# Unused matmuls ahead of the last block, and a kernel's last 64 columns in a bank of their own

## The chip, the cores and the metric

The kernel runs on one core of a Trainium2 chip. The metric is the device time of one execution in microseconds (us). Before the change the median of three runs is 773.96 us (773.9 to 774.07).

## The reference

One decode step of a parallel block: attention with cached keys and values, and a feed-forward net, both on the same normalised input, summed with the input. Two batch rows, model width 1024, 32 query heads on 4 key/value heads of width 128, 32768 cached positions, feed-forward width 3584, all in f32:

```python
xn = _layernorm(x)
q  = (xn @ wq)                              # 2 x 32 heads x 128
p  = softmax(q . k_cache * 128 ** -0.5)     # over 32768 positions, 8 heads share one k, v
a  = (p . v_cache) @ wo                     # 4096 -> 1024
h  = silu(xn @ w1)                          # 1024 -> 3584
return x + a + h @ w2                       # 3584 -> 1024
```

## The kernel before

Every weight and cache element is used for at most a few rows, so the program is a stream of 331 MB through three SBUF buffers (bufA, bufB, bufC, each 128 x 16384 f32), issued by SyncE (SP) in one fixed order, with TensorE following. First come wq and w1 (query and hidden activations), then eight turns of a TensorE loop (one for each pair of key/value head and batch row) over keys and values, and last wo and w2, which this change concerns.

In this last stage the reduction over 4096 + 3584 = 7680 inputs is cut into 60 tiles of 128 inputs, numbered t = 0 to 59: 32 of wo (weights oT from the attention), 28 of w2 (weights hT). Each tile has 128 x 1024 weights. Tiles 0 to 15 lie in bufA, 16 to 31 in bufC, 32 to 47 in bufB, and 48 to 59 in bufA again. The stationary operand is 32 columns wide (two batch rows, padded), so a matmul fills one group of 32 output partitions, and several matmuls with different groups are in the array together.

`tiles()` (from L351) goes through a block. Up to t = PAIRED - 1 a tile is *paired*: it is cut into two halves of 512 columns, even tiles go to groups 0 and 1, odd ones to groups 2 and 3 of the PSUM bank acc2 = ps[0]. After tile PAIRED - 1 VectorE adds these sums to the input x into ob (L363). From t = PAIRED on a tile is cut into four quarters of 256 columns (QW), one for each group of the bank acc. The sums in ob are folded into acc by four matmuls with a 0/1 matrix (fold), which wait for VectorE.

The last tile, t = 59, comes in four transfers of 128 KB, each with 64 columns of all four quarters; w2 is laid out on the host so that each is contiguous. TensorE waits for each. Then ScalarE copies acc (128 x 256) to SBUF (L388), issues the store of every sixteenth row (8 rows of 1 KB, L389), waits for it and clears the semaphores (L393).

The order of the work is that of the written program on each engine; engines wait for each other on semaphores (`pe.wait`, `act.wait`, `sp.wait_ge`). SP issues the last eight transfers into bufA once TensorE is through with bufA's wo block.

Of the kernel before, what the change touches and what calls it, by code (L numbers as in the profile page):

```python
# [3 lines left out]
F32 = mybir.dt.float32  # L4
# [4 lines left out]
B, HQ, HKV, SK, DH, D, F = 2, 32, 4, 32768, 128, 1024, 3584  # L9
P = 128  # L10
REP = HQ // HKV
W = 16384
# [4 lines left out]
FT = F // P  # L17
QW = D // 4
# [36 lines left out]
def gqa_plus_mlp_kernel(nc, x, kt, v, wq, wo, w1, w2, out):  # L55


    pe, dve, act, pool = (Stream(nc, e, n) for e, n in
                          ((nc.tensor, "pe"), (nc.vector, "dve"), (nc.scalar, "act"), (nc.gpsimd, "pool")))
    sp = nc.sync  # L60
    sems = [pe.sem, dve.sem, act.sem, pool.sem]

    def sem(name):
        sems.append(nc.alloc_semaphore(name))
        return sems[-1]

    def sb(name, *shape):
        return nc.alloc_sbuf_tensor(name, shape, F32).ap()

    def bank(name):  # L70
        return nc.alloc_psum_tensor(name, (P, 512), F32).ap()

    bufA, bufB, bufC = (sb(n, P, W) for n in ("bufA", "bufB", "bufC"))
    ldA, ldB, ldC, ldx, ldr, done = (sem(n) for n in ("ldA", "ldB", "ldC", "ldx", "ldr", "done"))
    tq, tps, trm, tgd, te, tls, tob = (sem(n) for n in ("tq", "tps", "trm", "tgd", "te", "tls", "tob"))
    ident, ones, sel, fold = sb("ident", P, P), sb("ones", P, P), sb("sel", P, 32), sb("fold", P, 64)
# [7 lines left out]
    oT, hT = sb("oT", P, HQ, 32), sb("hT", P, FT, 32)  # L84
    pre, sig, rsig = (sb(n, P, FT, B) for n in ("pre", "sig", "rsig"))
    pr = [sb(f"pr{i}", P, 512) for i in range(2)]
    ob, ot = sb("ob", P, 512), sb("ot", P, QW)
# [4 lines left out]
    pair = [nc.alloc_psum_tensor(f"ps{i}", (P, 1024), F32).ap() for i in range(NC)]  # L92
    ps = [pair[a // 2][:, a % 2 * 512:(a % 2 + 1) * 512] for a in range(2 * NC)]
    po, acc, smA, smB = (bank(n) for n in ("po", "acc", "smA", "smB"))
    acc = acc[:, :QW]

    def mm(o, lhsT, rhs, start=True, stop=True):
        return nc.tensor.matmul(o, lhsT, rhs, start=start, stop=stop)  # L98
# [26 lines left out]
    for i in range(2):  # L125
        t = dve.mark(V.bn_stats(stats[:, i, :], xt[:, i * 512:(i + 1) * 512]))
    dve.wait(t)
    t = dve.mark(V.bn_aggr(mv, stats))
    var, std, y0, t0, t1, rstd = (ln[:, i:i + 1] for i in range(6))
    dve.wait(t)  # L130
    t = dve.mark(V.tensor_scalar_add(var, mv[:, 1:2], EPS))
    act.wait(t)
    t = act.mark(nc.scalar.activation(std, var, AF.Sqrt))
    for f in (lambda: V.reciprocal(y0, std), lambda: V.tensor_mul(t0, y0, y0), lambda: V.tensor_mul(t1, t0, var),
# [4 lines left out]
        t = dve.mark(f())  # L139
    dve.wait(i_ident)  # L140
    i_sel = dve.mark(V.tensor_reduce(sel, ident.rearrange("p (g m) -> p m g", g=4), AX.X, ALU.add))
    i_fold = dve.mark(V.tensor_add(fold, ident[:, :64], ident[:, 64:]))
    pe.wait(t, i_ident)
    px = smA[:, :KT * B].rearrange("p (k b) -> p k b", b=B)
    for k in range(KT):
        m = mm(px[:, k, :], xn[:, k * P:(k + 1) * P], ident[:B, :B])
    t = pe.mark(m)
# [57 lines left out]
    def load(buf, src, s, *ticks):  # L205
        for of, n in ticks:
            sp.wait_ge(of.sem, n)
        sp.dma_start(buf, src).then_inc(s, 16)  # L208
# [5 lines left out]
    t = act.mark(nc.scalar.activation(sig, pre, AF.Exp, scale=-1.0))  # L214
    for f in (lambda: V.tensor_scalar_add(sig, sig, 1.0), lambda: V.reciprocal(rsig, sig),
              lambda: V.tensor_mul(hT[:, :, ::16], pre, rsig)):
        dve.wait(t, zs)
        t = dve.mark(f())
# [6 lines left out]
    start = pe.n  # L225
# [21 lines left out]
    for it in range(LOOPS):  # L247
        h, b = divmod(it, B)
        for c in range(NC):
            dve.wait(tick(it, c))  # L250
            t = dve.mark(V.transpose(st[:, 2 * c:2 * c + 2].rearrange("p a j m -> p (a j m)"), pair[c]))  # L251
            dve.wait(t)
            m = V.tensor_reduce(mx[:, c, :], st[:, 2 * c:2 * c + 2].rearrange("p a j (r m) -> p m (a j r)", r=4),  # L253
                                AX.X, ALU.max)
            if c == 0:
                m.then_inc(tps, 1)
        m = dve.mark(m)
# [5 lines left out]
        t = dve.mark(V.tensor_reduce(gm, smA[:REP, :P], AX.X, ALU.max))  # L263
# [3 lines left out]
        t = dve.mark(V.tensor_copy(gmax[:, 0, :], smB[:, :REP]))  # L267
# [6 lines left out]
        for c in range(NC):  # L274
            dve.wait(tick(it, 4 + c))
            m = V.tensor_reduce(ls[:, c, :], e8[c].rearrange("p n m -> p m n"), AX.X, ALU.add)  # L276
# [6 lines left out]
        t = dve.mark(V.reciprocal(rl, smA[:, :REP]))  # L283
# [8 lines left out]
    with nc.tensor.While(lambda: nc.tensor.snap(turn) < LOOPS):  # L292
        pe.take(tq)
        for a in range(4):
# [4 lines left out]
            for r in range(4):  # L299
                for q4 in range(4):  # L300
                    n = (4 * (a % 2) + q4) * 4 + r
                    m = mm(ps[a][32 * q4:32 * q4 + 32, :], qT[:, 32 * r:32 * r + 32], buf[:, n * 512:(n + 1) * 512],
                           r == 0, r == 3)
# [6 lines left out]
        for a in range(4):  # L310
# [4 lines left out]
            for j in range(16):  # L315
                q4, n = j % 4, 16 * (a % 2) + j
                m = mm(po[32 * q4:32 * q4 + 32, :], st[:, a, j, :], buf[:, n * 512:(n + 1) * 512],
                       a == 0 and j < 4, a == 3 and j >= 12)
# [5 lines left out]
        for r in range(4):  # L324
            m = mm(smB[:, :REP], ob[:, r * P:(r + 1) * P], sel[:, REP * r:REP * (r + 1)], r == 0, r == 3)
# [8 lines left out]
    def stream(buf, src, cuts, *ticks):  # L334

        for lo, hi in zip(cuts, cuts[1:]):
            s = sem(f"piece{len(pieces)}")
            load(buf[:, lo:hi], src[:, lo:hi], s, *ticks)
            pieces.append((hi, s))
            yield hi, s  # L340

    lo = 11 * D
# [3 lines left out]
        (bufB, [*stream(bufB, w2[:, :W], (0, 11 * D, W), tick(LOOPS - 1, 5))], 32),  # L346
    ]
    acc2 = ps[0]
    PAIRED = 56

    def tiles(buf, ends, at, n):  # L351
        for i in range(n):
            pe.wait((next(s for hi, s in ends if hi >= (i + 1) * D), 16))
            t = at + i
            lhsT, w = oT[:, t, :] if t < HQ else hT[:, t - HQ, :], buf[:, i * D:(i + 1) * D]
            if t < PAIRED:
                for half in range(2):
                    g = 2 * (t % 2) + half
                    m = mm(acc2[32 * g:32 * g + 32, :], lhsT, w[:, half * 512:(half + 1) * 512],
                           t < 2, t >= PAIRED - 2)  # L360
                if t == PAIRED - 1:
                    dve.wait(pe.mark(m), (ldr, 32))
                    i_sums = dve.mark(V.tensor_add(ob, acc2, xres))  # L363
            else:
                if t == PAIRED + 2:
                    pe.wait(i_fold, i_sums)
                    for j in range(4):
                        mm(acc[32 * j:32 * j + 32, :], fold[:, 32 * (j // 2):32 * (j // 2) + 32],
                           ob[:, (j % 2) * QW:(j % 2 + 1) * QW], False, False)
                for j in range(4):  # L370
                    m = mm(acc[32 * j:32 * j + 32, :], lhsT, w[:, j * QW:(j + 1) * QW], t == PAIRED, False)
        return m

    pe.wait(i_oT, i_hT)
    i_wo0 = pe.mark(tiles(*plan[0], 16))
    ends = [*stream(bufA, w2[:, W:], (0, 6 * D, 8 * D, 9 * D, 10 * D, lo, lo + QW, lo + 2 * QW, lo + 3 * QW,
                                      lo + D), i_wo0)]
    for buf, loaded, at in plan[1:]:
        tiles(buf, loaded, at, 16)
    tiles(bufA, ends, 48, 11)  # L380
    f = QW // 4
    for u in range(4):
        pe.wait((ends[5 + u][1], 16))
        for j in range(4):
            m = mm(acc[32 * j:32 * j + 32, u * f:(u + 1) * f], hT[:, FT - 1, :],
                   bufA[:, lo + (4 * u + j) * f:lo + (4 * u + j + 1) * f], False, u == 3)
    act.wait(pe.mark(m))
    act.wait(act.mark(nc.scalar.copy(ot, acc)))  # L388
    nc.scalar.dma_start(out, ot[::16, :]).then_inc(done, 16)  # L389
    act.wait((done, 16))  # L390
    first_sem = min(s.num for s in sems)
    assert sorted(s.num for s in sems) == list(range(first_sem, first_sem + len(sems)))
    nc.scalar.sem_clear(range(first_sem, first_sem + len(sems)))  # L393


# [27 lines left out]
```

## Time and profile before

| | us |
|---|---|
| median of 3 runs | 773.96 |
| the profiled execution | 773.65 |
| its span, first to last instruction | 772.2 |
| TensorE matmul busy | 386.6 (50%) |
| VectorE busy | 120.7 (16%) |
| ScalarE busy | 27.3 (4%) |
| data moved | 331.48 MB, mean 429 GB/s |

A row of a timeline reads: start, length, engine, line, operation, what it writes and reads, shape, number of records merged (x), and in brackets the idle time of the engine before it and what ended it. PE is TensorE's matmuls, PEld its weight loads, DVE VectorE, ACT ScalarE, a q behind a name the engine's sequencer. Line 98 is the helper that issues every matmul, so matmuls are told apart by the tiles that they write and read. The granted clock is the share of full speed at which TensorE runs.

### The profile page before, as it was taken

What the parts mean: (1) busy time and instruction counts of PE and PEld (TensorE: products, weight loads), DVE (VectorE), ACT (ScalarE), POOL (GpSimd) and SP (SyncE); (2) the same over time, 40 slices, a digit from 0 to 9 for tenths busy, and PEclk for the clock granted to TensorE, in tenths of its full rate; (3) what the DMA queues carried; (4) which work ended last, traced back from release to release, by engine and by line L of the source; (5) the groups of instructions that cost most, each with busy time, mean ns of one, the idle gap of its engine ahead of it and who ended that gap; (6) DMA issues with size and microseconds to landing.
All of it is one profiled execution on the core that took longest, in us unless ns stands there. A gap on an engine that the chain in (4) does not pass through costs nothing. (4 is left out here: it accounts for less than half of the span.)

```text
span 772.2 us, 5903 instructions
## 1 busy us (share of the span) xinstructions
PE 386.6 (50%) x2736; PEld 122.7 (16%) x2736; DVE 120.7 (16%) x153; ACT 27.3 (4%) x33; POOL 3.0 (0%) x10
## 2 busy tenths in 40 slices
PE   1545645554545444645454545444645454545466
PEld 1111211111111111211111111111211111111112
DVE  2000013111311131113111311131113111311000
ACT  0000101000100010001000000010001000000000
POOL 1000000000000000000000000000000000000000
PEclk9977677677677677677677677677677677677679
DMA  9999999999999999999999999999999999999997
GB/s 384 435 435 435 431 435 435 435 435 435 435 435 435 435 435 431 431 435 435 435 431 431 435 435 435 435 435 435 435 435 435 435 431 435 435 435 435 421 417 321
DMA packets 7091, 331.48 MB, mean 429 GB/s; under 512 B 798, under 2 KB 1318, under 8 KB 1708
## 3 DMA queue, kind: packets, MB, share of 16 engines
q1 hardware_dynamic: 7056, 331.35, 99.4%
q8 instruction: 6, 0.10, 0.0%
q10 hardware_dynamic: 28, 0.02, 0.0%
q14 instruction: 1, 0.01, 0.0%
HBM read 331.37 MB, written 0.01 MB: 429 GB/s over the span
## 5 line engine op out<-in xcount | busy, mean ns | idle before, releaser
L98 PE MATMUL ps<-bufB,qT 128*32 128x512 f32 x512 | 72.7, 731 | 83.2 <-PEq L52 83.2
L98 PE MATMUL po<-bufB,st 128*32 128x512 f32 x512 | 71.5, 721 | 82.7 <-PEq L52 82.7
L98 PE MATMUL ps<-bufA,qT 128*32 128x512 f32 x512 | 71.7, 723 | 53.1 <-PEq L52 53.1
L98 PE MATMUL po<-bufA,st 128*32 128x512 f32 x512 | 72.2, 727 | 39.3 <-PEq L52 39.3
L276 DVE TENSOR_REDUCE ls<-st 128x8 f32<-128x1024 f32 x16 | 31.8, 1984 | 229.6 <-PE po L98 229.6
L251 DVE STREAM_TRANSPOSE st<-ps 128x1024 f32<-128x1024 f32 x16 | 20.0, 1250 | 250.6 <-PE ps L98 250.6
L98 PEld LDWEIGHTS ps<-bufB,qT 128*32 128x32 f32 x512 | 20.0, 131 | 136.0 <-issue 136.0
L98 PEld LDWEIGHTS po<-bufB,st 128*32 128x32 f32 x512 | 19.7, 130 | 134.5 <-issue 134.5
L98 PEld LDWEIGHTS ps<-bufA,qT 128*32 128x32 f32 x512 | 19.8, 130 | 98.4 <-issue 98.4
L98 PEld LDWEIGHTS po<-bufA,st 128*32 128x32 f32 x512 | 19.9, 131 | 85.0 <-issue 85.0
L253 DVE TENSOR_REDUCE mx<-st 128x8 f32<-128x1024 f32 x16 | 31.7, 1981 | 0.6
L273 ACT ACTIVATE st<-st 128x1024 f32<-128x1024 f32 x16 | 16.9, 1056 | 358.7 <-DVE st L272 358.0
L98 PE MATMUL ps<-bufB,xnT 128*32 128x512 f32 x112 | 18.3, 730 | 14.8 <-PEq L52 14.8
L272 DVE TENSOR_TENSOR st<-st,gmax 128x1024 f32<-128x1024 f32 x16 | 18.9, 1222 | 0.3
L98 PE MATMUL smA<-ident,rm 128*8 128x128 f32 x16 | 3.7, 317 | 29.5 <-PEq L52 29.5
L98 PE MATMUL ps<-bufC,xnT 128*32 128x512 f32 x64 | 8.6, 698 | 10.8 <-DMA bufC<-in_w 10.8
L98 PE MATMUL ps<-bufC,oT 128*32 128x512 f32 x64 | 8.5, 692 | 9.7 <-DMA bufC<-in_wo 9.7
L281 ACT COPY ob<-po 128x512 f32<-128x512 f32 x8 | 4.7, 585 | 236.7 <-PE po L98 236.7
L98 PE MATMUL smA<-lsum,ones 128*128 128x8 f32 x16 | 3.3, 278 | 19.2 <-PEq L52 19.2
L98 PE MATMUL ps<-bufA,oT 128*32 128x512 f32 x64 | 9.6, 766 | 6.6 <-DMA bufA<-in_wo 6.6
L98 PE MATMUL ps<-bufA,xnT 128*32 128x512 f32 x64 | 9.7, 773 | 5.0 <-PEq L52 5.0
L98 PE MATMUL ps<-bufB,hT 128*32 128x512 f32 x64 | 8.9, 702 | 4.8 <-DMA bufB<-in_w 4.8
(65 smaller groups left out, 102.1 us busy)
## 6 DMA issues: line engine op xcount, KB each, us to landing
bufB<-in_w SPq DMA_DIRECT2D x1, 6144.0 KB, 26.2
bufB<-in_w SPq DMA_DIRECT2D x1, 5632.0 KB, 42.7
bufA<-in_w SPq DMA_DIRECT2D x1, 3072.0 KB, 36.3
bufB<-in_w SPq DMA_DIRECT2D x1, 2560.0 KB, 48.5
bufA<-in_w SPq DMA_DIRECT2D x3, 512.0 KB, 40.0
bufA<-in_w SPq DMA_DIRECT2D x1, 1024.0 KB, 38.4
bufA<-in_w SPq DMA_DIRECT2D x4, 128.0 KB, 38.0
bufA<-in_kt SPq DMA_DIRECT2D x8, 29.3
```

Of the source, the lines that this page charges most:

```text
L98: return nc.tensor.matmul(o, lhsT, rhs, start=start, stop=stop)
L251: t = dve.mark(V.transpose(st[:, 2 * c:2 * c + 2].rearrange("p a j m -> p (a j m)"), pair[c]))
L253: m = V.tensor_reduce(mx[:, c, :], st[:, 2 * c:2 * c + 2].rearrange("p a j (r m) -> p m (a j r)", r=4), AX.X, ALU.max)
L272: act.wait(dve.mark(V.tensor_sub(e8[c], e8[c], gmax.to_broadcast([P, 128, REP]))))
L273: nc.scalar.activation(e8[c], e8[c], AF.Exp, scale=SCALE).then_inc(te, 1)
L276: m = V.tensor_reduce(ls[:, c, :], e8[c].rearrange("p n m -> p m n"), AX.X, ALU.add)
L281: nc.scalar.copy(ob, po).then_inc(tob, 1)
```

## The change

Five edits, all in the last stage:

1. Between the block in bufB (tiles 32 to 47) and the last block in bufA, a TensorE loop of eight turns issues two matmuls a turn. Each multiplies 32 columns of the identity with pr[0] (128 x 512, f32) into partitions 0 to 31 of ps[2]. Nothing reads the result.
2. PAIRED is 57 in place of 56: tile 56 is paired as well. The fold matmuls stand ahead of tile 58, as before, but now ahead of that tile's wait for its transfer.
3. The 256 columns of a quarter are cut 192 + 64 (CUT = 192). Columns 0 to 191 go to acc, 192 to 255 to a second bank, smB (used by the attention before). Each quarter of tiles 57 and 58 and of the fold is thus two matmuls.
4. The last tile comes in two transfers, of 384 KB (the first 192 columns of each quarter) and 128 KB (the last 64). After the matmuls of each ScalarE copies that part.
5. SP issues the store, waits for it and clears the semaphores, in place of ScalarE. It stores every eighth row (16 rows), and the host takes every second of those.

```diff
-    PAIRED = 56
+    PAIRED, CUT = 57, 3 * QW // 4
+    banks = [(acc, 0, CUT), (smB, CUT, QW)]
+
+    def singly(j, lhsT, w, start=False):
+        for bank, a, e in banks:
+            mm(bank[32 * j:32 * j + 32, :e - a], lhsT, w[:, a:e], start, False)
 
     def tiles(buf, ends, at, n):
         for i in range(n):
+            t = at + i
+            if t == PAIRED + 1:
+                pe.wait(i_fold, i_sums)
+                for j in range(4):
+                    singly(j, fold[:, 32 * (j // 2):32 * (j // 2) + 32], ob[:, (j % 2) * QW:(j % 2 + 1) * QW])
             pe.wait((next(s for hi, s in ends if hi >= (i + 1) * D), 16))
...
             else:
-                if t == PAIRED + 2:
-                    pe.wait(i_fold, i_sums)
-                    for j in range(4):
-                        mm(acc[32 * j:32 * j + 32, :], fold[:, 32 * (j // 2):32 * (j // 2) + 32],
-                           ob[:, (j % 2) * QW:(j % 2 + 1) * QW], False, False)
                 for j in range(4):
-                    m = mm(acc[32 * j:32 * j + 32, :], lhsT, w[:, j * QW:(j + 1) * QW], t == PAIRED, False)
+                    singly(j, lhsT, w[:, j * QW:(j + 1) * QW], t == PAIRED)
...
-    ends = [*stream(bufA, w2[:, W:], (0, 6 * D, 8 * D, 9 * D, 10 * D, lo, lo + QW, lo + 2 * QW, lo + 3 * QW,
-                                      lo + D), i_wo0)]
+    ends = [*stream(bufA, w2[:, W:], (0, 6 * D, 8 * D, 9 * D, 10 * D, lo, lo + 4 * CUT, lo + D), i_wo0)]
     for buf, loaded, at in plan[1:]:
         tiles(buf, loaded, at, 16)
+
+
+    again = nc.tensor.alloc_register("again")
+    nc.tensor.reg_mov(again, 0)
+    with nc.tensor.While(lambda: nc.tensor.snap(again) < 8):
+        for i in range(2):
+            mm(ps[2][:32, :], ident[:, :32], pr[0])
+        nc.tensor.reg_add(again, again, 1)
     tiles(bufA, ends, 48, 11)
-    f = QW // 4
-    for u in range(4):
-        pe.wait((ends[5 + u][1], 16))
+    for (hi, landed), (bank, a, e) in zip(ends[5:], banks):
+        pe.wait((landed, 16))
         for j in range(4):
-            m = mm(acc[32 * j:32 * j + 32, u * f:(u + 1) * f], hT[:, FT - 1, :],
-                   bufA[:, lo + (4 * u + j) * f:lo + (4 * u + j + 1) * f], False, u == 3)
-    act.wait(pe.mark(m))
-    act.wait(act.mark(nc.scalar.copy(ot, acc)))
-    nc.scalar.dma_start(out, ot[::16, :]).then_inc(done, 16)
-    act.wait((done, 16))
+            at = lo + 4 * a + j * (e - a)
+            m = mm(bank[32 * j:32 * j + 32, :e - a], hT[:, FT - 1, :], bufA[:, at:at + e - a], False, True)
+        act.wait(pe.mark(m))
+        i_ot = act.mark(nc.scalar.copy(ot[:, a:e], bank[:, :e - a]))
+    sp.wait_ge(act.sem, i_ot[1])
+    sp.dma_start(out, ot[::8, :]).then_inc(done, 16)
+    sp.wait_ge(done, 16)
```

How the instructions stand on TensorE around the last block: first before, from the end of bufB's block (waits in brackets; pieceN is the semaphore of a transfer, dve is VectorE's).

```order
L98 MATMUL ps<-bufB,hT 32x512 x9
L98 MATMUL ps<-bufA,hT 32x512 [waits piece4]
L98 MATMUL ps<-bufA,hT 32x512 x11
L98 MATMUL ps<-bufA,hT 32x512 [waits piece5]
L98 MATMUL ps<-bufA,hT 32x512 x3
L98 MATMUL acc<-bufA,hT 32x256 [waits piece6]
```

The same place in the changed program:

```order
L97 MATMUL ps<-bufB,hT 32x512 x9
L386 UNCONDITIONAL_BRANCH
L386 COMPARE_AND_BRANCH
L97 MATMUL ps<-pr,ident 32x512 x2
L389 REGISTER_ALU
L386 UNCONDITIONAL_BRANCH
L97 MATMUL ps<-bufA,hT 32x512 [waits piece4]
L97 MATMUL ps<-bufA,hT 32x512 x11
L97 MATMUL ps<-bufA,hT 32x512 [waits piece5]
L97 MATMUL ps<-bufA,hT 32x512 x3
L97 MATMUL ps<-bufA,hT 32x512 [waits piece6]
L97 MATMUL ps<-bufA,hT 32x512
```

The loop (its body is run eight times) stands between bufB's last matmul and the wait for piece4, and tile 56 has become two paired matmuls behind piece6. At the end of ScalarE's program, before, there stood the copy, the store and the clearing of semaphores:

```order
L388 COPY ot<-acc 128x256
L389 DMA out_y<-ot 8x256
L393 ISA
```

Now ScalarE ends with two copies

```order
L397 COPY ot<-acc 128x192
L397 COPY ot<-smB 128x64
```

and SP's program ends with two transfers for the last tile in place of four, the store and the clearing:

```order
L207 DMA bufA<-in_w 128x768
L207 DMA bufA<-in_w 128x256
L399 DMA out_y<-ot 16x256
L403 ISA
```

More of the change, by code (lines that the diff above doesn't have):

```diff
@@ L94, in gqa_plus_mlp_kernel @@
     po, acc, smA, smB = (bank(n) for n in ("po", "acc", "smA", "smB"))
-    acc = acc[:, :QW]
     def mm(o, lhsT, rhs, start=True, stop=True):
@@ L348, in gqa_plus_mlp_kernel @@
     acc2 = ps[0]
-    PAIRED = 56
+    PAIRED, CUT = 57, 3 * QW // 4
[3 more added lines that the diff above has]
+            mm(bank[32 * j:32 * j + 32, :e - a], lhsT, w[:, a:e], start, False)
     def tiles(buf, ends, at, n):
         for i in range(n):
+            t = at + i
[3 more added lines that the diff above has]
+                    singly(j, fold[:, 32 * (j // 2):32 * (j // 2) + 32], ob[:, (j % 2) * QW:(j % 2 + 1) * QW])
             pe.wait((next(s for hi, s in ends if hi >= (i + 1) * D), 16))
-            t = at + i
             lhsT, w = oT[:, t, :] if t < HQ else hT[:, t - HQ, :], buf[:, i * D:(i + 1) * D]
@@ L375, in gqa_plus_mlp_kernel @@
     i_wo0 = pe.mark(tiles(*plan[0], 16))
-    ends = [*stream(bufA, w2[:, W:], (0, 6 * D, 8 * D, 9 * D, 10 * D, lo, lo + QW, lo + 2 * QW, lo + 3 * QW,
-                                      lo + D), i_wo0)]
+    ends = [*stream(bufA, w2[:, W:], (0, 6 * D, 8 * D, 9 * D, 10 * D, lo, lo + 4 * CUT, lo + D), i_wo0)]
     for buf, loaded, at in plan[1:]:
         tiles(buf, loaded, at, 16)
+    again = nc.tensor.alloc_register("again")
[4 more added lines that the diff above has]
+        nc.tensor.reg_add(again, again, 1)
     tiles(bufA, ends, 48, 11)
-    f = QW // 4
-    for u in range(4):
-        pe.wait((ends[5 + u][1], 16))
+    for (hi, landed), (bank, a, e) in zip(ends[5:], banks):
+        pe.wait((landed, 16))
         for j in range(4):
-            m = mm(acc[32 * j:32 * j + 32, u * f:(u + 1) * f], hT[:, FT - 1, :],
-                   bufA[:, lo + (4 * u + j) * f:lo + (4 * u + j + 1) * f], False, u == 3)
-    act.wait(pe.mark(m))
-    act.wait(act.mark(nc.scalar.copy(ot, acc)))
-    nc.scalar.dma_start(out, ot[::16, :]).then_inc(done, 16)
-    act.wait((done, 16))
+            at = lo + 4 * a + j * (e - a)
[5 more added lines that the diff above has]
+    sp.wait_ge(done, 16)
     first_sem = min(s.num for s in sems)
     assert sorted(s.num for s in sems) == list(range(first_sem, first_sem + len(sems)))
-    nc.scalar.sem_clear(range(first_sem, first_sem + len(sems)))
+    sp.sem_clear(range(first_sem, first_sem + len(sems)))
 def kernel(A_x, A_k_cache, A_v_cache, A_wq, A_wo, B_x, B_w1, B_w2):
@@ L413 @@
     last = arrays["w2"][:, -D:]
-    last[:] = lay(last, (P, 4, 4, QW // 4), (0, 2, 1, 3), (P, D))
+    groups, cut = last.reshape(P, 4, QW).copy(), 3 * QW // 4
+    last[:, :4 * cut], last[:, 4 * cut:] = groups[:, :, :cut].reshape(P, -1), groups[:, :, cut:].reshape(P, -1)
     nc = bacc.Bacc("TRN2", target_bir_lowering=False, num_devices=1, dynamic_dma_scratch_size=2048)
@@ L417 @@
             for k, a in arrays.items()]
-    args.append(nc.dram_tensor("out_y", (4 * B, QW), F32, kind="ExternalOutput").ap())
+    args.append(nc.dram_tensor("out_y", (16, QW), F32, kind="ExternalOutput").ap())
     gqa_plus_mlp_kernel(nc, *args)
     r = run_bass_kernel_spmd(nc, [{f"in_{k}": a for k, a in arrays.items()}], core_ids=[0])
-    y = r.results[0]["out_y"].reshape(4, B, QW).transpose(1, 0, 2)
+    y = r.results[0]["out_y"].reshape(4, 4, QW)[:, ::2].transpose(1, 0, 2)
     return np.ascontiguousarray(y).reshape(B, 1, D)
```

## The prediction

> **What bounds the kernel now.** I read the page first, then the chain that ended last, then the timeline of the last 40 us. The page says that the transfers are busy nearly everywhere and TensorE half of the time:
>
> ```profile
> span 772.2 us, 5903 instructions
> PE 386.6 (50%) x2736; PEld 122.7 (16%) x2736; DVE 120.7 (16%) x153; ACT 27.3 (4%) x33; POOL 3.0 (0%) x10
> DMA  9999999999999999999999999999999999999997
> ```
>
> Nothing in the change touches the first 757 us, so only the end counts. The chain there (start, length, what):
>
> ```profile
> 727.30 40.85 DMA bufA<-in_w
> 768.16 0.04 issue
> 768.20 1.65 PE acc L98 x48
> 769.85 0.02 issue
> 769.87 0.37 ACT ot L388
> ```
>
> Weights land until 768.16 and a little after, TensorE works 1.65 us behind them, ScalarE copies, and the store takes the rest. The timeline shows what TensorE does before (a matmul is two records here: the page counts x64 for 32 matmuls of a 16-tile block):
>
> ```profile
> 748.45 8.92 PE L98 MATMUL ps<-bufB,hT 128*32 128x512 f32 x64 [4.83 <-DMA bufB<-in_w]
> 761.84 5.34 PE L98 MATMUL ps<-bufA,hT 128*32 128x512 f32 x32 [4.47 <-DMA bufA<-in_w]
> 762.64 0.21 PEld L98 LDWEIGHTS ps<-bufA,hT 128*32 128x32 f32 x4 [0.64 <-issue]
> 763.49 0.21 PEld L98 LDWEIGHTS ps<-bufA,hT 128*32 128x32 f32 x4 [0.64 <-issue]
> 766.14 0.13 PEld L98 LDWEIGHTS ps<-bufA,hT 128*32 128x32 f32 x4 [0.30 <-issue]
> 766.57 0.13 PEld L98 LDWEIGHTS acc<-bufA,hT 128*32 128x32 f32 x4 [0.30 <-issue]
> 766.99 1.05 PE L98 MATMUL acc<-bufA,hT 128*32 128x256 f32 x16
> ```
>
> TensorE ends bufB at 748.45 + 8.92 = 757.37 and waits 4.47 us, until 761.84, for the first piece of bufA. It then goes in rounds of four records, one for each group of 32 output partitions. A round is 0.85 us long at first (762.64 to 763.49) and 0.43 us later (766.14 to 766.57). The clock explains that:
>
> ```profile
> 755.10:758.50 3.40, 2.27 (x22) 0.76 (x14) 0.00 (x0) 0.00 (x0) 0.00 (x0) 1.00 0.99 426
> 758.50:761.90 3.40, 0.06 (x4) 0.06 (x8) 0.00 (x0) 0.00 (x0) 0.00 (x0) 1.00 0.93 393
> 761.90:765.30 3.40, 3.40 (x20) 0.84 (x24) 0.00 (x0) 0.00 (x0) 0.00 (x0) 0.51 1.00 406
> ```
>
> (Columns: window, length, PE, PEld, DVE, ACT, POOL busy, granted clock, DMA share, GB/s.) After the almost empty window 758.5 to 761.9 the clock is halved for one window.
>
> **What the 16 unused matmuls cost.** They stand on TensorE between bufB's last matmul and the wait for bufA. All 16 write the same 32 partitions (ps[2][:32]), 512 columns each, in f32. So they are 32 records in one group, and the question is how long a lone record takes. No lone 512-column stream is in the trace; two kinds of rows bound it:
>
> ```profile
> 77.11 2.78 PE L98 MATMUL ps<-bufB,xnT 128*32 128x512 f32 x9 [5.03 <-PEq L52]
> 128.89 0.38 PE L98 MATMUL smA<-ident,rm 128*8 128x128 f32 x2 [3.68 <-PEq L52]
> 206.85 0.59 PE L98 MATMUL smA<-ident,rm 128*8 128x128 f32 x2 [3.68 <-PEq L52]
> ```
>
> The first: with three groups in place of four, at half clock, nine records are three rounds, and 2.78 us is again two steps of 0.85 us and a last record of 1.06 us. A round gets no shorter when a group is missing. The last two are one lone matmul of 128 columns, at full and at half clock: 0.38 and 0.59 us. If a record streams at t per 128 columns, two take 2t at full clock and 4t at half, and the difference 0.21 us gives t = 0.105 us. That is 0.42 us for 512 columns, the length of the full round. So a lone group is no faster than four together: 0.43 us a record, 0.86 us a matmul. The lower bound is a lone record at half of that (0.21 us, if the four groups shared what limits a round; the three-group row speaks against it); the upper bound is 0.85 us, at half clock. I take 0.43 us, the row it is nearest to: 32 x 0.43 = 13.8 us. The wait that should hold them is 4.47 us.
>
> The Trainium skill (FP8 and Floating Point Precision, TensorE Precision Notes) has an f32 product as four passes through the array. Its page TensorE: Matmul & The Clock Gate (Back-to-back issue gap) gives a warm stream of 512 columns as about 216 ns. Taken as the price of each of the 16 matmuls the latter makes 3.5 us, which fits into the wait, and the kernel would end near 773.3 us; four such passes make 0.86 us, and with these the trace agrees.
>
> **The sum.** The last record of bufB ends at 757.37; a record is about 0.16 us longer than its stream (0.38 us less two of 0.105 us), so the group is free at about 757.2. The unused matmuls end at 757.2 + 13.8 = 771.0, 9.2 us after bufA's first piece landed (761.84). PAIRED = 57 makes nine paired tiles of two matmuls: eight tiles are eight full rounds, the ninth has two rounds to itself, 10 x 0.43 = 4.3 us at full clock (the unused matmuls have kept it). They end at 775.3, the last round starts at 774.8. Then VectorE's sum, which the fold matmuls wait for:
>
> ```profile
> 766.56 0.61 PE L98 MATMUL ps<-bufA,hT 128*32 128x512 f32 x4
> 767.24 0.69 DVE L363 TENSOR_TENSOR ob<-ps,xres 128x512 f32<-128x512 f32 x1 [57.69 <-PE ps L98]
> 768.20 0.64 PE L98 MATMUL acc<-ob,fold 128*32 128x256 f32 x8 [0.16 <-DMA bufA<-in_w]
> 769.87 0.37 ACT L388 COPY ot<-acc 128x256 f32<-128x256 f32 x1 [63.60 <-PE acc L98]
> 770.27 0.65 ACTq L389 DMA_DIRECT2D out_y<-ot  x1
> ```
>
> From the last paired round (766.56) to the sum's end (767.93) it was 1.37 us; the fold then started at 768.20, behind a landing at 768.16, so the hop alone is between 0.04 and 0.27 us; I take 0.15. Fold now at 774.8 + 1.5 = 776.3. What hid this sum before, two tiles of 0.43 us, is one tile now; it makes the fold late by nothing more than the 1.5 us above. From the fold to the end it was 772.2 - 768.2 = 4.0 us. Afterwards the columns per group are the same (fold, tile 58, last tile), cut 192 + 64. The short matmuls have no floor that shows:
>
> ```profile
> L98 PE MATMUL acc<-bufA,hT 128*32 128x256 f32 x24 | 1.7, 379 | 0.0
> L98 PE MATMUL acc<-bufA,hT 128*32 128x64 f32 x32 | 0.7, 222 | 0.0
> ```
>
> Sixty-four columns cost 222 - 160 = 60 ns and 256 cost 379 - 160 = 220 ns. The last landings fall away as a limit (they are long there), a gain of up to 0.1 us.
>
> The ScalarE copies: 512 columns took 585 ns and 256 took 372 ns, so 0.83 ns a column, and 64 columns take some 0.21 us in place of 0.37 us. But the copy of 192 columns (0.32 us) starts only 0.2 us earlier, since in a TensorE-bound end its matmuls are just before; of the 0.16 us about 0.06 us is left. The store moves from ScalarE's queue to SP's:
>
> ```profile
> L281 ACT COPY ob<-po 128x512 f32<-128x512 f32 x8 | 4.7, 585 | 236.7 <-PE po L98 236.7
> 725.51 19.85 SPq L208 DMA_DIRECT2D bufA<-in_w  x8
> ```
>
> SP issues its eight late pieces until 745.4 (now seven) and then has nothing but this store, so nothing queues behind its new wait. Sixteen rows in place of eight, one queue in place of another: the whole old tail from the copy's end (770.24) to 772.2 is 1.96 us, of which the issue is 0.65. I put the store between 0.3 us shorter and 0.3 us longer, and take 0.1 us shorter. So from the fold on 3.8 us in place of 4.0.
>
> End of span 776.3 + 3.8 = 780.1, against 772.2: 7.9 us more. The profiled execution took 773.65 us, so 781.6; the median of the three runs is 773.96, 0.3 us above it. I put 781.7 us, 1.0% slower. The merits of the other edits (an earlier last transfer, a shorter last copy, tile 56 paired) are some 0.3 us and lie behind a TensorE that is 8 us late.
>
> **Rivals.**
>
> *A lone group does not hold the clock.* In the row below TensorE is at work for 1.07 of 3.5 us with all groups, and the next window is at half clock:
>
> ```profile
> 202.10:205.60 3.50, 1.07 (x12) 0.14 (x4) 2.33 (x2) 0.00 (x0) 0.00 (x0) 0.99 1.00 431
> 205.60:209.00 3.40, 1.15 (x4) 0.61 (x4) 1.78 (x6) 0.00 (x0) 0.00 (x0) 0.50 1.11 482
> ```
>
> The unused matmuls fill all the time but a quarter of the groups. If what counts is the share of the array, 0.25 is below that window's and the clock halves at 761.9. Until then 11 records are done; 21 remain at 0.85 us, to 779.8. The paired rounds start cold, three or four of them until a full window is over, then 0.43 us: some 785.5 in place of 775.3. The sum is 10.2 us more, 792 us. Against it: 100% of the time at work is no gap. The Trainium skill (TensorE: Matmul & The Clock Gate, What's actually happening) halves the clock after an idle window of about 3.4 us and speaks of time, not of share. By that rule the clock holds and 781.7 stands; the windows above agree with it as far as all-group matmuls go, and no run here shows a lone group.
>
> *The unused matmuls are cheap* (the other side). Before, the paired rounds ended at 766.99; ten at full clock take 4.3 us, so TensorE may start bufA as late as 762.7 and lose nothing. From 757.2 that is 5.5 us, 0.34 us a matmul: below this they are covered and pay back, above it each us is lost. At 0.21 us a record they end at 757.2 + 6.9 = 764.1, 1.4 us past that point: 773.96 + 1.4 less 0.3 and the landing's 0.1 makes 775.0, not slower by what can be told. Cheaper still, the last landing near 769.4 still sets the end and only the 0.3 us of copy and store is won: 773.5. For it speaks that no row shows a lone 512-column stream; against it the two 128-column rows and the three-group row.
>
> *The loop's turns drain TensorE.* If each of the eight turns waits until its two matmuls are out, 0.16 us of tail and some 0.3 us of branch (the main loop's branch is 169 ns, twice a turn) come on top, 8 x 0.5 = 4 us: 785.7 us.
>
> ```profile
> L292 PEldq COMPARE_BRANCH  x17: 76/169/218, 87.8 to 708.7; - x17
> 708.23 1.04 PE L98 MATMUL smB<-sel,ob 128*128 128x8 f32 x8
> ```
>
> Against it: the last branch of the main loop starts at 708.7, while the matmuls ahead of it run to 709.27; it does not wait for them.
>
> **How the numbers follow.** Forecast 57%, half clock 27%, draining turns 5%, cheap matmuls 11%. A measurement of this kernel tells 0.2% (1.5 us) from no change. Only the cheap case is not slower, and its gain of 0.3 to 0.5 us cannot reach 1.5 us: faster 1%, same 10%, slower 89%. The forecast's own range is 780 to 783.5 (hop, store and record length 0.42 to 0.45 us); the slower cases reach 792, so the range is 779.5 to 793, which leaves out the cheap case and a little.
>
> **What would show it.** The timeline should have the unused matmuls as 32 records over 13.8 us from about 757.2, the wait for bufA gone, the first matmul of bufA near 771 at clock 1.00, the fold near 776.3, the copies at 777.5 to 778, the span near 780. Unused matmuls over by 764, or a TensorE wait on bufA still there, prove the price wrong; a granted clock of 0.50 from 761.9 on while they run proves the first rival. The store's share shows between the end of the second copy and the end of the span: 1.96 us before.

## The result and the profile after

The changed kernel takes 782.08 us (median of 5 runs, 781.16 to 783.55), against 773.96 us before: a ratio of 1.0103, 95% interval 1.0091 to 1.0114. It is 1.0% slower. The profiled execution took 781.43 us, its span 780.1 us.

The chain that ended last, in the changed kernel (start, length, what), no longer ends in a transfer into bufA. The last transfer in it is bufB's, and from 748.75 on it is TensorE nearly alone:

```profile
706.35 42.36 DMA bufB<-in_w
748.71 0.04 issue
748.75 26.81 PE ps L97 x130
775.56 0.02 issue
775.58 0.70 DVE ob L371
776.29 0.04 issue
776.33 0.56 PE acc L97 x8
...
777.82 0.43 ACT ot L397 x2
```

The timeline of the changed kernel shows what TensorE does in these 26.81 us, once it is through with bufB's block:

```profile
757.34 13.47 PE L97 MATMUL ps<-pr,ident 128*32 128x512 f32 x31
770.22 0.63 PE L97 MATMUL ps<-bufA,hT 128*32 128x512 f32 x3
770.64 0.59 PE L97 MATMUL ps<-pr,ident 128*32 128x512 f32 x1
770.68 4.85 PE L97 MATMUL ps<-bufA,hT 128*32 128x512 f32 x33
775.58 0.69 DVE L371 TENSOR_TENSOR ob<-ps,xres 128x512 f32<-128x512 f32 x1 [64.33 <-PE ps L97]
776.33 0.56 PE L97 MATMUL acc<-ob,fold 128*32 128x192 f32 x8 [0.31 <-DVE ob L371]
777.82 0.32 ACT L397 COPY ot<-acc 128x192 f32<-128x192 f32 x1 [70.88 <-PE acc L97]
778.03 0.22 ACT L397 COPY ot<-smB 128x64 f32<-128x64 f32 x1
778.28 0.55 SPq L399 DMA_DIRECT2D out_y<-ot  x1
```

The unused matmuls run one after the other, 31 of their 32 records from 757.34 to 770.81 (13.47 us) and the last to 771.23 (it has a row of its own). The wait for bufA is gone: its first matmul starts at 770.22, 8.4 us after it did before. The group of the unused matmuls in the same trace, and the stages (window, length, PE, PEld, DVE, ACT, POOL busy, granted clock, DMA share, GB/s):

```profile
L97 PE MATMUL ps<-pr,ident 128*32 128x512 f32 x32 | 13.9, 592 | 0.0
758.50:761.90 3.40, 3.40 (x9) 0.88 (x8) 0.00 (x0) 0.00 (x0) 0.00 (x0) 1.00 0.95 401
761.90:765.30 3.40, 3.40 (x9) 0.88 (x8) 0.00 (x0) 0.00 (x0) 0.00 (x0) 1.00 1.00 405
765.30:768.80 3.50, 3.50 (x9) 0.88 (x8) 0.00 (x0) 0.00 (x0) 0.00 (x0) 1.00 0.79 307
768.80:772.20 3.40, 3.40 (x24) 1.01 (x26) 0.00 (x0) 0.00 (x0) 0.00 (x0) 1.00 0.02 5
```

The clock stays at full speed through all of it, and in the last row almost nothing is transferred any more (5 GB/s): the weights have landed while TensorE is still at matmuls that nobody reads.

### The profile page after: what moved, and what is told of

It is laid out like the page before. It is cut to its first block, busy times and chain, and to the rows that moved or that the text cites. A ratio compares the mean times of both kernels' runs of the same rounds, so it can differ in the third digit from the quotient of the medians.

```text
span 780.1 us, 6008 instructions
## 1 busy us (share of the span) xinstructions
PE 401.0 (51%) x2772; PEld 128.0 (16%) x2772; DVE 120.7 (15%) x153; ACT 27.4 (4%) x34; POOL 3.0 (0%) x10
## 5 line engine op out<-in xcount | busy, mean ns | idle before, releaser
L97 PE MATMUL po<-bufB,st 128*32 128x512 f32 x512 | 73.1, 735 | 82.9 <-PEq L52 82.9
L97 PE MATMUL ps<-bufA,qT 128*32 128x512 f32 x512 | 73.3, 736 | 53.2 <-PEq L52 53.2
L97 PE MATMUL ps<-pr,ident 128*32 128x512 f32 x32 | 13.9, 592 | 0.0
```

## The experiments

Theory: the unused matmuls are the whole loss, because 16 in one group are 32 records of 0.43 us, 13.8 us in place of a wait of 4.47 us; TensorE may start bufA as late as 762.7 for nothing. Rivals: the loop or the mere number of matmuls, the changed tail (banks, copies, store), and a clock that goes by the share of the array.

The ratios are to runs of the kernel before that were taken beside each kernel; their medians lie between 773.95 and 774.18 us.

| kernel | median us | runs | ratio to before, 95% interval |
|---|---|---|---|
| changed | 782.08 | 5 | 1.0091 to 1.0114 |
| no unused matmuls | 774.87 | 11 | 0.9996 to 1.0014 |
| 16 over four groups | 773.46 | 11 | 0.9983 to 1.0001 |
| 6 in one group | 774.01 | 11 | 0.9990 to 1.0008 |
| 10 in one group | 776.11 | 7 | 1.0017 to 1.0039 |
| 16 in one group, no loop | 782.07 | 4 | 1.0089 to 1.0120 |
| before, with 16 over four groups | 774.13 | 11 | 0.9990 to 1.0008 |
| 6 of 32 rows x 8 | 776.52 | 10 | 1.0015 to 1.0048 |
| 16 over four groups, VectorE copies the last 64 | 773.46 | 11 | 0.9984 to 1.0002 |
| 10 of 32 rows x 32 | 782.18 | 4 | 1.0091 to 1.0126 |
| 10 of 128 rows x 8 | 776.51 | 7 | 1.0019 to 1.0042 |
| 16 over four groups, store as before | 773.80 | 11 | 0.9987 to 1.0005 |
| before, with SP's 16-row store | 773.71 | 11 | 0.9986 to 1.0004 |

**Without the unused matmuls.** Edit to the changed kernel:

```diff
-    with nc.tensor.While(lambda: nc.tensor.snap(again) < 8):
-        for i in range(2):
-            mm(ps[2][:32, :], ident[:, :32], pr[0])
-        nc.tensor.reg_add(again, again, 1)
```

> The changed kernel without the unused matmuls and their loop. Theory (the unused matmuls are the whole loss, because one column group takes 0.43 us a record): TensorE waits for bufA again until about 761.8 and starts at half clock; ten paired rounds end near 767.9, the fold starts near 768.9, 0.7 us later than in the kernel before, and copy and store give 0.2 us back: 774.3 us (773.7 to 774.9), the clock 0.50 from 761.9. Rival (the split banks, the two copies and SP's store cost several us): it stays above 777.

Measured 774.87 us: 7.2 us of the 8.1 us are gone with the loop, and what is left of the change cannot be told from the kernel before. It is 0.6 us above the forecast. The timeline and the stages say why:

```profile
762.01 7.09 PE L97 MATMUL ps<-bufA,hT 128*32 128x512 f32 x36 [3.86 <-DMA bufA<-in_w]
758.50:761.90 3.40, 0.00 (x0) 0.00 (x0) 0.00 (x0) 0.00 (x0) 0.00 (x0) 0.79 0.94 398
761.90:765.30 3.40, 3.29 (x16) 0.79 (x20) 0.00 (x0) 0.00 (x0) 0.00 (x0) 0.50 1.01 406
765.30:768.80 3.50, 3.50 (x24) 0.93 (x17) 0.00 (x0) 0.00 (x0) 0.00 (x0) 0.71 0.77 303
```

The paired records end at 769.1, where the forecast had 767.9, because the clock stayed at half for a part of the third window too: 0.71, where the profile before had 0.99. How much of the last block is cold changes from one execution to the next; the spans of these 11 runs lie between 772.5 and 774.0 us.

**The same 16, spread over the four groups.**

```diff
-    with nc.tensor.While(lambda: nc.tensor.snap(again) < 8):
-        for i in range(2):
-            mm(ps[2][:32, :], ident[:, :32], pr[0])
+    with nc.tensor.While(lambda: nc.tensor.snap(again) < 4):
+        for i in range(4):
+            mm(ps[2][32 * i:32 * i + 32, :], ident[:, :32], pr[0])
```

> The changed kernel with the same 16 unused matmuls, four to each of the four groups of 32 output partitions in place of 16 to one (four turns of four matmuls). Theory: they are eight rounds of four records, 8 x 0.43 = 3.4 us, over at about 760.8 inside the wait; the clock holds, the paired rounds end near 766.2, the last landing near 769.4 sets the end: 773.4 us (772.9 to 774.0). Rival (any 16 unused matmuls of 512 columns cost 13.8 us, whatever their group): 781.5.

Measured 773.46 us, as the theory had it, 8 us below the rival. Number, columns and operands are those of the changed kernel; only the output partitions differ, and the loop has four turns of four. Its timeline:

```profile
757.25 3.70 PE L97 MATMUL ps<-pr,ident 128*32 128x512 f32 x32
762.04 4.82 PE L97 MATMUL ps<-bufA,hT 128*32 128x512 f32 x36 [1.09 <-DMA bufA<-in_w]
769.31 0.53 PE L97 MATMUL acc<-bufA,hT 128*32 128x192 f32 x8 [0.30 <-DMA bufA<-in_w]
```

The same 32 records take 3.70 us in place of 13.9, TensorE waits 1.09 us for bufA again, and the last tile waits for its transfer. Thirty-six paired records now take 4.82 us, at full clock (1.00), where 32 took 5.34 before. All 11 runs (773.33 to 773.64) lie below all 29 runs of the kernel before that were taken beside them (773.72 to 774.99), though the interval just includes 1.

**Six and ten in one group**, three and five turns of the loop in place of eight.

> The changed kernel with 6 unused matmuls in one group in place of 16 (three turns). Theory: 12 records x 0.43 = 5.2 us, over at about 762.4, before the point 762.7 from which each us is lost, and the clock holds: 773.4 us (772.9 to 774.2). Rival (the loop itself, not the matmuls' length, delays the last block): above 776.

> The changed kernel with 10 unused matmuls in one group (five turns). Theory: 20 records x 0.43 = 8.6 us, over at about 765.8; six matmuls of 0.86 us less than 16, so 5.2 us below the changed kernel's 781.4 to 782.1: 776.6 us (775.9 to 777.3). Rival (a fixed delay, whatever the number): 781.

Measured 774.01 and 776.11 us. Six end at 762.66 and cost nothing beside the kernel before; ten cost 2.1 us more than six, and sixteen 6.0 us more than ten, 0.99 us a matmul over the last six against 0.86 us forecast (0.85 us a matmul by the two profiled spans, 775.0 and 780.1, and by the lowest times, 776.06 and 781.16). Their timelines, six first:

```profile
757.35 5.31 PE L97 MATMUL ps<-pr,ident 128*32 128x512 f32 x12
762.17 4.82 PE L97 MATMUL ps<-bufA,hT 128*32 128x512 f32 x36
```

```profile
757.22 8.32 PE L97 MATMUL ps<-pr,ident 128*32 128x512 f32 x19
765.40 4.85 PE L97 MATMUL ps<-bufA,hT 128*32 128x512 f32 x33
```

With six, TensorE comes out of them when bufA lands; with ten it is 3.2 us late. So there is a free allowance and a slope beyond it, not a fixed delay. The median with six is still 0.6 us above its forecast and above the spread version. Eight of its 11 spans are 772.1 to 772.4 us, about those of the spread version (772.0 to 772.3); the other three are longer, up to 773.6, and the time outside the span is longer too (median 1.51 us against 1.35, with two executions at 2.4 and 2.5). Why is not shown.

**Sixteen without the loop**, written out one after the other.

> The changed kernel with its 16 unused matmuls in one group written out one after the other, without the loop. Theory (the array's time is the price, the loop's branches lie beside it): the 32 records still take 13.7 us, as with the loop: 781.6 us (780.8 to 782.6). Rival (the loop's turns add time): 778 or below.

Measured 782.07 us, the changed kernel's time to 0.01 us. The loop costs nothing beside the array: its 32 records have the same row as with the loop.

```profile
L97 PE MATMUL ps<-pr,ident 128*32 128x512 f32 x32 | 13.9, 593 | 0.0
```

**The kernel before with the spread matmuls alone.**

> The kernel before with the sixteen unused matmuls over four groups as the only edit (tail, banks, transfers and store as before). Theory: TensorE starts the last block at full clock and is through with its paired tiles about 1.7 us earlier, but the fold waits for the transfer that lands at 768.2 and the last piece lands at 769.4, so nothing is won on a good execution: 773.8 us (773.4 to 774.2), the fold still near 768.2. Rival (the end is set by TensorE's cold start): 772.3 or below.

Measured 774.13 us; the median did not move. The end of the chain of this run is the same as before, a landing and then TensorE:

```profile
726.86 41.49 DMA bufA<-in_w
768.36 0.04 issue
768.40 1.66 PE acc L98 x48
770.06 0.02 issue
770.09 0.37 ACT ot L394
```

The paired records are done by 765.7, 1.5 us sooner, and the fold waits for its transfer all the same (768.40). What the full clock does change is the spread: the spans of the 11 runs lie between 772.3 and 772.6 us, those of 27 runs of the kernel before between 772.2 and 773.5. In six of the 11, however, the time outside the span is longer than in any of those 27 (1.66 to 2.90 us against 1.43 to 1.56), so the median of the times understates what the warm start does inside the span; the cause stays open.

In the kernel before, TensorE's cold start sets the end in some executions, and the landing in the others. The profile before (span 772.2) shows the second. The first is in the profile of the kernel before with SP's store, the last of the kernels under the next heading (span 772.9). There the clock was 0.74 in the third window, VectorE's sum ended at 768.91, and the fold follows it with no wait for a transfer:

```profile
765.30:768.80 3.50, 3.50 (x36) 1.00 (x28) 0.58 (x1) 0.00 (x0) 0.00 (x0) 0.74 0.83 305
769.06 0.64 PE L98 MATMUL acc<-ob,fold 128*32 128x256 f32 x8
```

**The store.** Two kernels: the changed tail with the spread matmuls but ScalarE's 8-row store, and the kernel before with SP's 16-row store.

> The changed kernel with the sixteen unused matmuls over four groups, but with the store as before: ScalarE issues it, eight rows. Theory (the split banks, the later last matmuls and the shorter last copy win what that kernel won, the store 0.1 us): 773.6 us (773.3 to 773.9). Rival (the sixteen-row store on SP's queue wins most of it): 774.0 or above.

> The kernel before with the store alone changed: SP issues it, sixteen rows. Theory (the store is worth 0.1 us): 774.0 us (773.6 to 774.3), with the spread of the kernel before, about 1.2 us. Rival (the store wins most of what the changed tail wins, and narrows the spread): 773.6 or below.

Measured 773.80 and 773.71 us. Both lie inside the theory's range, between its number and the rival's: the store is worth some 0.3 us (773.46 against 773.80; 773.95 against 773.71 beside the same runs), more than the 0.1 us of the theory, and does not narrow the spans by much (772.2 to 773.1). From the last copy's end to the span's end it is 1.95 us with ScalarE's store and 1.87 with SP's, the 0.1 us of the theory; the rest lies outside the span (time less span 1.43 to 1.60 us with ScalarE's store, 1.28 to 1.35 with SP's, over these 22 runs). What is shorter there no trace shows. Of the 0.7 us of the spread version 0.3 are thus the store's. What the warm block and the split tail win together is less sure: 0.4 us as the rest of the 0.7, but 0.15 us by the kernel with ScalarE's store against the runs beside it (773.80 against 773.95, an interval that includes 1). These runs do not part the two.

**VectorE copies the last 64 columns.**

```diff
-        act.wait(pe.mark(m))
-        i_ot = act.mark(nc.scalar.copy(ot[:, a:e], bank[:, :e - a]))
+        if bank is acc:
+            act.wait(pe.mark(m))
+            i_ot = act.mark(nc.scalar.copy(ot[:, a:e], bank[:, :e - a]))
+        else:
+            dve.wait(pe.mark(m))
+            i_o2 = dve.mark(V.tensor_copy(ot[:, a:e], bank[:, :e - a]))
```

> The changed kernel with the sixteen unused matmuls over four groups, and the last 64 columns copied by VectorE in place of ScalarE, so that the second copy need not wait for the first. Theory (the last landing sets the end, then matmuls, copies and store in a row): ScalarE's first copy ends 0.1 to 0.2 us before its second one did, VectorE's ends before that, so 0.1 to 0.2 us below the same kernel with two ScalarE copies: 773.3 us (772.9 to 773.7). Rival: the wait for two engines or VectorE's own start takes it back, 773.5 or above.

Measured 773.46 us, inside the range but the same as with two ScalarE copies: the gain of 0.1 to 0.2 us is not there.

```profile
769.65 0.32 ACT L398 COPY ot<-acc 128x192 f32<-128x192 f32 x1 [63.63 <-PE acc L97]
769.77 0.23 DVE L401 COPY ot<-smB 128x64 f32<-128x64 f32 x1 [2.38 <-PE smB L97]
770.08 0.55 SPq L404 DMA_DIRECT2D out_y<-ot  x1
```

The two copies end together (769.97 and 770.00), since the wide one starts only 0.12 us before the narrow one. From the start of the wide copy to the end of the last one it is 0.35 us, against 0.44 with two ScalarE copies (769.91 to 770.35), but the store is issued 0.08 us behind the last copy in place of 0.02. So the wait for two engines, the rival, takes back most of the 0.09 us won.

**What keeps the clock.** A fourth of the array had held it; three kernels ask what counts. First six matmuls of 32 input rows and 8 output partitions.

> The changed kernel with 6 unused matmuls (three turns), each with 8 output partitions from 32 input rows in place of 32 from 128: 1/64 of the array, the same 512 columns. If the clock goes by the time at work: 12 records in 5.2 us, the clock 1.00 from 758.5 to the end, as with six full ones, 773.6 us (773.0 to 774.2). If it goes by the share of the array: 0.50 from about 762 on, the paired rounds at 0.85 us for one or two windows, 774.9 us (774.2 to 775.5).

Measured 776.52 us, with the widest spread of all, 773.98 to 779.29. The clock went down while TensorE was at work all the time:

```profile
758.50:761.90 3.40, 3.40 (x9) 0.68 (x8) 0.00 (x0) 0.00 (x0) 0.00 (x0) 1.00 0.94 398
763.60:767.00 3.40, 3.40 (x20) 0.86 (x16) 0.00 (x0) 0.00 (x0) 0.00 (x0) 0.50 1.01 402
```

So time at work alone does not hold it. The time is above both forecasts; in the profiled execution the store also took 1.2 us longer than elsewhere (3.05 us from the last copy to the end), which has no explanation here, and neither has the spread of the spans, 772.7 to 778.0. Then ten matmuls of the two shapes of a sixteenth of the array, one new line in each of two kernels:

```diff
-            mm(ps[2][:32, :], ident[:, :32], pr[0])
+            mm(ps[2][:32, :], ident[:32, :32], pr[0][:32, :])      # 32 rows x 32
+            mm(ps[2][:8, :], ident[:, :8], pr[0])                  # 128 rows x 8, the other kernel
```

> The changed kernel with 10 unused matmuls (five turns) of 32 input rows by 32 output partitions, in place of 128 by 32: a sixteenth of the array. The ten with 128 rows held the clock at 1.00 and took 776.1 us. If what counts is the columns or the time at work, the same: 776.1 us (775.6 to 777.3), clock 1.00 through 758 to 772. If it is the rows or the product of both, the clock halves at a window's end between 760.2 and 763.6, and the rest of the unused matmuls takes twice as long: 779 to 787 us.

> The same with 10 unused matmuls of 128 input rows by 8 output partitions: also a sixteenth of the array. If what counts is the rows or the time at work: 776.1 us (775.6 to 777.3), clock 1.00. If it is the columns or the product, the clock halves between 760.2 and 763.6: 779 to 787 us.

Measured 782.18 us with 32 rows and 776.51 us with 128 rows. The matmuls of 32 rows and the stages of the two, 32 rows first:

```profile
757.53 12.12 PE L97 MATMUL ps<-pr,ident 32*32 32x512 f32 x20
758.50:761.90 3.40, 3.40 (x10) 0.81 (x9) 0.00 (x0) 0.00 (x0) 0.00 (x0) 1.00 0.94 396
761.90:765.30 3.40, 3.40 (x7) 0.73 (x6) 0.00 (x0) 0.00 (x0) 0.00 (x0) 0.63 1.01 410
765.30:768.80 3.50, 3.50 (x6) 0.57 (x4) 0.00 (x0) 0.00 (x0) 0.00 (x0) 0.50 0.76 298
```

```profile
758.50:761.90 3.40, 3.40 (x9) 0.72 (x8) 0.00 (x0) 0.00 (x0) 0.00 (x0) 1.00 0.94 395
761.90:765.30 3.40, 3.40 (x12) 0.78 (x14) 0.00 (x0) 0.00 (x0) 0.00 (x0) 1.00 1.00 406
765.30:768.80 3.50, 3.50 (x34) 1.04 (x28) 0.00 (x0) 0.00 (x0) 0.00 (x0) 1.00 0.78 305
```

With few rows the clock halves, and the 20 records take 12.12 us in place of the 8.7 us of 128 rows (757.22 to 765.96); with few columns it does not. In these runs the input rows at work count, not the output columns.

## Why the prediction was right

*The price of a lone record* was the term on which everything hung, 0.43 us by the difference of two short rows. Measured: 31 records in 13.47 us, less 0.16 us at the end, 0.43 us each. The spread kernel shows the other half: the same records in four groups take a fourth. The Trainium skill (TensorE: Matmul & The Clock Gate, Back-to-back issue gap) gives about 216 ns as the gap of a single warm matmul of 512 columns, and about 131 ns in a sustained stream. Neither is the price of these f32 matmuls, which take 0.86 us in the trace, four times 216 ns. This fits the four passes that the Trainium skill (FP8 and Floating Point Precision, TensorE Precision Notes) has for an f32 product; the trace shows two records a matmul and not the passes themselves.

*The sum* came out nearly term by term: unused matmuls over at 771.0 (measured 771.23 with the last record's tail, 771.1 without), paired records over at 775.3 (775.53), fold at 776.3 (776.33), end of span 780.1 (780.1). That the last two agree so closely is partly luck, since smaller errors cancel. BufB's first matmul came 0.3 us later in this execution (748.75 against 748.45), but the first unused record followed it by 8.59 us where the forecast had 8.75. The paired records ended 0.2 us late, but from the end of VectorE's sum (776.27) to the fold it was 0.06 us in place of 0.15.

*The clock* held, as the forecast and not its first rival had it, but not for the reason given there, that time at work is no gap: the ten matmuls of 32 rows were also at work all the time and lost it. That the unused matmuls had 128 input rows played no part in the forecast, so in this term it was right by luck. The row at 202.10, which the prediction counts for a rule of idle windows, shows less than that: TensorE was at work for 1.07 of the 3.50 us, so the clock went down after a window that was not idle.

*The point of no loss*, 762.7, was borne out by six (nothing lost beside the kernel before) and ten matmuls (2.1 us more than six). *The draining loop* is refuted by the written-out kernel. *The other edits* were put at some 0.3 us behind a late TensorE; with TensorE on time the store alone is worth that. Inside the span it is the 0.1 us of the forecast (1.87 us from the last copy to the end in the changed kernel, 1.95 before); the part outside the span was not in the sum at all.

*The median* (782.08) is 0.4 us above the forecast of 781.7, within the runs' own spread.

## What to carry to other kernels

Work that fills a wait has to be priced against the wait, by its own shape: here 16 matmuls into one group of 32 partitions took 13.9 us and 16 into four groups 3.7, and each matmul beyond the point from which the next block is late cost its full length. When a warm-up makes TensorE early, look at what it waits for next: here a landing took back most of the 1.5 us, and what was left showed in the spread between executions and not in the median. The price of a lone stream, which no row showed, was had here from two rows of the same short operation at two clocks, whose difference leaves out what both rows share.

## What the runs showed of the hardware that was not expected

In these runs the granted clock goes neither by the time at work nor by the share of the array. Matmuls of 128 rows by 32 columns and 128 by 8 held it at 1.00, a fourth and a sixteenth of the array; 32 by 32, also a sixteenth, and 32 by 8 let it fall to 0.50 with TensorE at work throughout. The Trainium skill (TensorE: Matmul & The Clock Gate, What's actually happening) speaks of busy and idle windows alone and does not say what counts as busy. If time at work did, none of the four would have lost the clock; the traces of the two with 32 rows show that it does not. Each of the last three shapes was profiled once, and other numbers of rows were not tried.

SP's store of 16 rows is 0.08 us shorter than ScalarE's of 8 inside the span, and leaves another 0.2 us less outside it; the two differ in queue, rows and issuing engine, and which of these it is was not tried. In the kernel with six unused matmuls and in the kernel before with the spread ones, some executions (two and three of 11) have 2.1 to 2.9 us outside the span, where most others have 1.3 to 1.7; the cause stays open.
